# Attention by pairs of sequences, and token groups cut across all four sequences, in a fused attention and expert kernel

## The chip, the cores and the metric

The kernel runs on one core of one Trainium2 chip. The metric is device time in microseconds (us), from the first to the last instruction. All data are FP32. Lines such as L843 are line numbers of the kernel before.

## The reference

A decayed linear attention over blocks of a sequence feeds four experts that every token goes through, weighted by normalised probabilities. Cut to what matters:

```python
# q, k, v: (4, 8, 768, 64); lam: one decay per head
for b in range(nb):                                   # blocks of 64
    intra = einsum('bhic,bhjc->bhij', qb, kb) * Dmask     # lam ** (i - j), 0 above the diagonal
    out[:, :, sl] = einsum('bhij,bhjd->bhid', intra, vb) + einsum('bhid,bhde->bhie', qb * lam_pow, kv_state)
    kv_state = lam_block * kv_state + einsum('bhsd,bhse->bhde', kb * rev_pow, vb)
x = out.transpose(0, 2, 1, 3).reshape(3072, 512)      # token = sequence * 768 + position
p = domain_probs / (domain_probs.sum(-1, keepdims=True) + 1e-9)
for e in range(4):                                    # w1: (4, 512, 1024), w2: (4, 1024, 512)
    y += p[:, e:e + 1] * (maximum(x @ w1[e], 0) @ w2[e])
```

Sequences don't touch each other in attention, and tokens don't touch each other in the experts. So the tokens may be grouped in any way, as long as a sequence's chunks come in order.

## The kernel before

**Chunks and groups.** Attention uses chunks of 128 positions (C), six to a sequence (NCH), 24 in all. The kernel numbers them n = sequence * 6 + chunk. Eight consecutive chunks make a token group of 1024 tokens (CPG = 8, G = 1024), three groups in all (NG). A group's attention output lies turned in the tile xT, and the experts work on it while attention of the next group runs in between. The first group is sequence 0 and two chunks of sequence 1, and so on.

**Attention of a chunk** has three steps on TensorE. `turn(n)` transposes q and k of 8 heads (8 transposes, L529) into PSUM, ScalarE copies them out; from the second chunk of a sequence on, VectorE also scales q by the decay (qs). GpSimd decays k (`decayed`). `scores(n)` makes k q^T for 8 heads (L551), with two products side by side on 64 rows each, into two PSUM banks; VectorE masks them with the decay (two instructions, st<-sp). `values(n)` adds the state's part (L574, not for a first chunk), the values (L579) and makes the chunk's addition to the state (L587, not for a last chunk). These use halves of the array too. ScalarE copies the result into xT, VectorE updates the state kv, one for the sequence in hand. A product over FP32 is two records in the profile, so 8 products are 16 records; a transpose is one.

For eight of the chunks (`turn_across`), q and k are first re-laid in DRAM by small DMAs (`bring_across`, pieces let go one at a time by `trickle`, tensor across), so that VectorE's 32x32 transposes suffice and TensorE has nothing to turn.

**The experts** are products by a seven-multiplication scheme (M1 to M7) in two levels. A unit is one group with one expert, 12 in all; for each unit of the loop (`at`), `second_product` (L897, banks q..) of the present unit and `first_product` (L843, banks g1 and g3) of the next run interleaved in seven steps i, each in eight slots x. In the order SEQ the first products are M1, M5, M6, M2, M7, M3, M4. Each of the seven inner products of a first product fills g1 or g3 with four records, and VectorE (in M1 and M5 for four of them ScalarE) adds it to the tiles m; the next inner product into that bank waits for this. The last group (LAST) uses another nesting (L1123).

**What sets the order.** The schedule is manual: instructions run on each engine in the order written. Work of VectorE that is not urgent, sums of blocks above all, goes on the list `background`; `rest()` takes one item in each slot. Before, attention's VectorE work (masks, scaling, state) is put at the front of the same list by `soon`; in the first group it is done at once. Attention's steps lie in a list from which one is taken at x == 5 of each step and in some at x == 2 (L1483). `pump` lets out GpSimd's weight preparation (`chores`) and DMA stores at a pace; `feed` and `feed2` load operands on SyncE's queue a step or more ahead.

**Start and end.** The first group's attention has no experts to hide behind: a hand-written loop over i interleaves turn, scores and values of three consecutive chunks with first direct products (`direct_product`, L1253, tiles pM and pc). At the end, `give`, `give_across` and `turn_end` turn the last group's results back and store them.

**Memory.** Tiles of 128x512 for attention and experts share one pool of NPOOL = 47.

Of the kernel before, what the change touches and what calls it, by code (L numbers as in the profile page):

```python
# [17 lines left out]
NPOOL = 47  # L18
AHEAD = 2
# [3 lines left out]
def kernel(  # L23
# [30 lines left out]
    nc = tc.nc  # L54
# [53 lines left out]

    nat = {}

    def load(n, names="qkv"):

        b, c = divmod(n, NCH)
# [242 lines left out]
    ACROSS = {2: 2, 3: 2}  # L356
    across = dram.tile([B, 2, P, NHP, NCH * 4, 32], FP32, name="across")
    pieces = []

    def bring_across(b):  # L360
        c = ACROSS[b]
        for x, of in enumerate((q, k)):
            for y in range(4):
                for ac in range(NHP):
                    src = of[b, 4 * (y // 2) + ac, c * C:, (y % 2) * 32:(y % 2 + 1) * 32]
                    to = across[b, x, y * 32:(y + 1) * 32, ac, c * 4:]
                    pieces.append(lambda to=to, src=src: nc.sync.dma_start(
                        out=to, in_=src.rearrange("(t p) d -> p t d", p=32),
                    ))

    def trickle(m=1):
        for _ in range(m):
            if pieces:
                pieces.pop(0)()

    def comes_across(n):
        b, c = divmod(n, NCH)
        return b in ACROSS and c >= ACROSS[b]

    def load_across(n):  # L380
        b, c = divmod(n, NCH)
        for x, name in enumerate("qk"):
            t = small(f"{name}x")
            nc.sync.dma_start(
                out=t[:].rearrange("p (h c) -> p h c", c=C),
                in_=across[b, x, :, :, c * 4:c * 4 + 4].rearrange("p h t d -> p h (t d)"),
            )
            nat[n, name + "x"] = t

    def load_more(n):  # L390
        if not comes_across(n):
            load(n)
        else:
            trickle(len(pieces))
# [5 lines left out]
    for n, names in ((0, "qk"), (1, "qk"), (0, "v"), (2, "qk"), (1, "v"), (3, "qk")):  # L400
        load(n, names)
    raw_w1(0, "A11")
    load(2, "v")
    load(3, "v")
# [39 lines left out]
    kv = consts.tile([P, NHP, D], FP32, name="kv")  # L444
# [17 lines left out]
    def turn_gates():  # L462
        p, o = bank("s0", "gp"), small("gr")
        n = CPG * E
        nc.tensor.transpose(out=p[0:n, 0:P], in_=gate[:, LAST * CPG:].rearrange("p n e -> p (n e)"), identity=ident[:])
# [9 lines left out]
    background = []  # L475
    aside = []
# [17 lines left out]
    def soon(n, *work):  # L494

        background[0:0] = work
        if n < CPG:
            rest(len(work))
# [7 lines left out]
    def turn_across(n):  # L506

        qT, kT, kn = nat.pop((n, "qx")), nat.pop((n, "kx")), nat[n, "k"]
        qs = small("qs") if n % NCH else None

        def scaled():
            if n % NCH:
# [4 lines left out]
        if n % NCH < NCH - 1:  # L517
            decayed(kn)

    def turn(n, tags):  # L520
# [15 lines left out]
        if n % NCH:  # L536
# [3 lines left out]
        if n % NCH < NCH - 1:  # L540
            decayed(kn)

    def scores(n, tags):
        while n not in turned:
            rest(force=True)
        qT, kT, _ = turned[n]

        sp = [bank(tags[r], "sp") for r in range(2)]
        for ac in range(NHP):
            for r in range(2):  # L550
                nc.tensor.matmul(  # L551
                    out=sp[r][:, ac * C:(ac + 1) * C], lhsT=hc(kT)[half[r], ac], rhs=hc(qT)[half[r], ac],
                    start=True, stop=True,
                )
        st = [small("st") for _ in range(2)]

        def mask(hd):
            tt(nc.vector, st[hd][:], sp[hd][:], s_decay[:, hd].rearrange("p h c -> p (h c)"), ALU.mult)

        soon(n, *(lambda hd=hd: mask(hd) for hd in range(2)))  # L560
        masked[n] = st

    def values(n, tags):
        kn, vn = nat.pop((n, "k")), nat.pop((n, "v"))
        qs = turned.pop(n)[2]
        st = masked.pop(n)
        c = n % CPG
        first, last = n % NCH == 0, n % NCH == NCH - 1

        op = [bank(tags[r], "op") for r in range(2)]  # L570
        heads = [(a, r, c) for a in range(2) for r in range(2) for c in range(2)]
        if not first:
            for a, r, x in heads:
                nc.tensor.matmul(  # L574
                    out=op[r][half[x], a * C:(a + 1) * C], lhsT=kv[half[r], 2 * a + x], rhs=hc(qs)[half[r], 2 * a + x],
                    start=(a == 0), stop=False, skip_group_check=True,
                )
        for a, r, x in heads:
            nc.tensor.matmul(  # L579
                out=op[r][half[x], a * C:(a + 1) * C], lhsT=vn[:, 4 * r + 2 * a + x], rhs=hc(st[r])[:, 2 * a + x],  # L580
                start=(first and a == 0), stop=True, skip_group_check=True,
            )
        kvp = op[1][:, 2 * C:].rearrange("p (h d) -> p h d", d=D)
        if not last:
            for ac in range(NHP):
                for r in range(2):
                    nc.tensor.matmul(  # L587
                        out=kvp[half[r], ac], lhsT=kn[:, 2 * ac + r], rhs=vn[:, 4 * r + ac], start=(ac == 0), stop=True,
                        skip_group_check=True,
                    )  # L590
        for r in range(2):
            nc.scalar.copy(
                out=xT[:, 2 * r:2 * r + 2, c * C:(c + 1) * C],
                in_=op[r][:, 0:2 * C].rearrange("p (a t) -> p a t", t=C),
            )
        if not last:
            def state():
                if first:
                    nc.vector.tensor_copy(out=kv[:], in_=kvp)
                else:  # L600
                    tt(nc.vector, kv[:], kv[:], q_decay[:, :, C - 1:C].to_broadcast([P, NHP, D]), ALU.mult)
                    tt(nc.vector, kv[:], kv[:], kvp, ALU.add)

            soon(n, state)

    def attention(g):

        steps = []
        early, late = prepare_x(g)
        for n in range(g * CPG, (g + 1) * CPG):  # L610
            steps.append(lambda n=n: turn(n, ("s0", "s1")))
            steps.append(lambda n=n: scores(n, ("s0", "s1")))

            def end(n=n):
# [3 lines left out]
                values(n, ("s0", "s1"))  # L618
                if n + AHEAD < B * NCH:
                    load_more(n + AHEAD)  # L620
                if n == g * CPG + CPG // 2 - 1:
                    chores[0:0] = early
                if n == g * CPG + CPG - 1:
                    chores.extend(late)
            steps.append(end)
        return steps


    hid = {}
# [44 lines left out]
    LAST = NG - 1  # L674
# [207 lines left out]
    def second_product(g, e, m, banks):  # L882

        def part(sj, s):
# [23 lines left out]
            o, x, w = a[:, j * DH:(j + 1) * DH], p[:, s * DH:(s + 1) * DH], gate[:, n, e:e + 1]  # L908
# [5 lines left out]
            if e == E - 1 and m in ("M2", "M4", "M5", "M3"):  # L914
                results.append(lambda: nc.sync.dma_start(out=out[n * P:(n + 1) * P, j * DH:(j + 1) * DH], in_=o))
# [91 lines left out]

    RESULT = {"M2": (0, 0), "M3": (0, 1), "M4": (1, 0), "M5": (1, 1)}

    def give(m, t, tags, dds=(0, 1)):  # L1010
# [5 lines left out]
        for x, dd in enumerate(dds):  # L1016
# [6 lines left out]
        r, d = LAST * G + j * W + t * 256, i * DH + dds[0] * P  # L1023
        nc.sync.dma_start(
            out=out[r:r + 256, d:d + w].rearrange("(s p) d -> p s d", p=P),
# [5 lines left out]
    def give_across(m, dd, t):  # L1031
# [7 lines left out]
        nc.vector.transpose(out=o[:, t * 256:(t + 1) * 256], in_=sums[m][:, 2 * dd + t])  # L1039
        r, d = LAST * G + j * W, i * DH + dd * P  # L1040
        for a in range(4 * t):
            by = nc.scalar if a == 1 else nc.sync
            by.dma_start(
                out=out[r:r + W, d + a * 32:d + (a + 1) * 32].rearrange("(b p) d -> p b d", p=32),
                in_=o[a * 32:(a + 1) * 32].rearrange("p (b d) -> p b d", d=32),
            )
# [40 lines left out]
    def turned_product(t, h, w):  # L1087
# [9 lines left out]
        r = LAST * G + j * W + t * 256  # L1097
# [420 lines left out]
```

## Time and profile before

| | |
|---|---|
| time, median of 3 runs (lowest, highest) | 1186.49 us (1186.17, 1189.06) |
| span of the profiled execution | 1183.3 us |
| granted TensorE clock | 1.000 |
| scores of all chunks, L551, records, busy | 256 + 128, 18.6 + 9.3 us |
| values, L579 | 384 records, 26.7 us |
| state's part, L574 | 320 records, 13.3 us |
| addition to the state, L587 | 320 records, 12.7 us |
| transposes of q and k, L529 | 128 records, 19.3 us |
| first products, L843, largest form | 1960 records, 469.8 us |
| masks st<-sp on VectorE | 48, mean 680 ns |
| scaling qs<-qT and qs<-qx | 12 of 938 ns, 8 of 791 ns |
| 128x512 sum on VectorE with one PSUM input, m<-pg,m | mean 687 ns |
| DMA engines' mean busy share between 90 and 560 us | 0.91 to 0.93 |

Busy is the time in which at least one record of the group was running; records overlap, so a matmul's length (mean 279 ns for L579) is more than the distance to the next. To see what a group costs TensorE, compare the start of its first record with the start of the first record after it. In the timeline, xN is the number of records merged into one line; brackets at the end of a line give idle time before it and what ended it, and a line without brackets had none.

### The profile page before, as it was taken

How to read it: one execution, taken by the hardware profiler on the slowest of the kernel's cores; microseconds unless marked ns; L12 is line 12 of the kernel's file. 1: busy time of each engine (PE TensorE's matmuls, PEld its weight loads, DVE VectorE, ACT ScalarE, POOL GpSimd, SP SyncE). 2: the span in 40 equal slices, each digit the busy share in tenths (PEclk: the TensorE clock that was granted, in tenths of full speed). 3: DMA queues.
4: the chain of work that ended last, by engine and by line, in shares of the span. 5: the costliest groups of instructions: out<-in, count | busy, mean ns of one | idle time of the engine just before them, and what ended most of it. 6: DMA issues, size and time to landing. Idle time of an engine off the chain costs nothing.

```text
span 1183.3 us, 17880 instructions
## 1 busy us (share of the span) xinstructions
PE 1175.7 (99%) x6559; PEld 1022.7 (86%) x6559; DVE 790.7 (67%) x1333; ACT 274.0 (23%) x500; POOL 628.7 (53%) x600
## 2 busy tenths in 40 slices
PE   9999999999999999999999999999999999999998
PEld 8888888888888888888888888888888888888887
DVE  6785785567468857647856774773665676777785
ACT  3332122112211201211220120121243342341331
POOL 2756258349457900055244655416584693783884
PEclk9999999999999999999999999999999999999999
DMA  9797799999999997899998989998986657566543
GB/s 232 194 292 238 250 300 310 362 326 333 353 359 334 328 291 227 262 287 303 303 317 247 295 287 318 275 312 294 316 289 238 261 196 272 212 237 248 213 155 95
DMA packets 265608, 324.23 MB, mean 274 GB/s; under 512 B 121489, under 2 KB 206897, under 8 KB 265521
## 3 DMA queue, kind: packets, MB, share of 16 engines
q1 hardware_dynamic: 254912, 320.27, 81.6%
q10 hardware_dynamic: 10608, 2.82, 1.1%
q8 instruction: 52, 0.85, 0.3%
q14 instruction: 36, 0.29, 0.1%
HBM read 237.69 MB, written 89.54 MB: 277 GB/s over the span
## 4 chain that ended last, share of the span: by engine, by line
PE 94%; DVE 3%; DMA 2%; issue 0%; POOL 0%; SPq 0%; ACT 0%; DVEq 0%
PE pg L843 38%; PE q L897 32%; PE pq L1123 13%; PE pM L1253 2%; PE op L579 2%; PE sp L551 2%; PE pc L1253 2%; DMA w_ops<-ops 2%; PE op L574 1%; PE op L587 1%; DVE sums L95 0%; PE qp L529 0%; PE kp L529 0%; PE pg L1123 0%; DVE acc L95 0%; DVE m L95 0%
## 5 line engine op out<-in xcount | busy, mean ns | idle before, releaser
L843 PE MATMUL pg<-xs_in,ws_in 128*128 128x256 f32 x1960 | 469.8, 380 | 0.9 <-DVE m L95 0.9
L843 PEld LDWEIGHTS pg<-xs_in,ws_in 128*128 128x128 f32 x1960 | 371.2, 190 | 52.9 <-DVE m L95 2.3
L95 DVE TENSOR_TENSOR m<-pg,m 128x512 f32<-128x512 f32 x451 | 308.1, 687 | 106.5 <-PE pg L843 99.6
L897 PE MATMUL q<-w2t,hS 128*128 128x256 f32 x1024 | 243.4, 380 | 0.0
L897 PEld LDWEIGHTS q<-w2t,hS 128*128 128x128 f32 x1024 | 193.2, 190 | 27.0 <-issue 0.2
L913 DVE SCALAR_TENSOR_TENSOR acc<-q,gate,acc 128x256 f32<-128x256 f32 x192 | 92.5, 482 | 170.2 <-PE q L897 170.0
L897 PE MATMUL q<-w2t,m 128*128 128x256 f32 x768 | 182.7, 381 | 0.0
L897 PEld LDWEIGHTS q<-w2t,m 128*128 128x128 f32 x768 | 144.8, 190 | 20.5 <-issue 0.3
L855 ACT ACTIVATE m<-m 128x512 f32<-128x512 f32 x132 | 83.0, 630 | 283.6 <-DVE m L95 276.6
L95 POOL TENSOR_TENSOR m<-m,xT 128x512 f32<-128x512 f32 x64 | 80.7, 1276 | 71.6 <-ACT m L855 53.9
L95 POOL TENSOR_TENSOR kn<-kn,s_decay 128x512 f32<-128x512 f32 x20 | 22.5, 1126 | 140.7 <-PE kp L529 134.8
L95 DVE TENSOR_TENSOR sums<-pq,sums 128x256 f32<-128x256 f32 x153 | 64.2, 422 | 46.0 <-PE pq L1123 38.8
L851 ACT COPY m<-pg 128x512 f32<-128x512 f32 x88 | 51.6, 586 | 174.3 <-PE pg L843 173.4
L1123 PE MATMUL pq<-acc,w2t 128*128 128x256 f32 x352 | 86.6, 379 | 0.0
L95 POOL TENSOR_TENSOR ops<-w2b 128x256 f32<-128x256 f32 x24 | 17.9, 766 | 119.4 <-DMA w2b<-in_moe_w_dram 111.3
L1123 PEld LDWEIGHTS pq<-acc,w2t 128*128 128x128 f32 x352 | 66.8, 190 | 9.3 <-issue 0.3
L95 POOL TENSOR_TENSOR acc<-hT,hT 128x512 f32<-128x512 f32 x32 | 40.3, 1274 | 30.3 <-PE pq L1123 28.4
L95 POOL TENSOR_TENSOR w2o<-w2b 128x512 f32<-128x512 f32 x32 | 40.6, 1291 | 23.3 <-DMA w2b<-in_moe_w_dram 23.3
L786 ACT ACTIVATE m<-m 128x512 f32<-128x512 f32 x44 | 27.7, 630 | 101.8 <-DVE m L95 101.8
L95 DVE TENSOR_TENSOR hS<-m,m 128x512 f32<-128x512 f32 x56 | 45.3, 812 | 4.9 <-ACT m L855 4.9
L95 DVE TENSOR_TENSOR m<-m,m 128x512 f32<-128x512 f32 x56 | 47.2, 844 | 0.0
L95 POOL TENSOR_TENSOR acc<-hT,acc 128x512 f32<-128x512 f32 x32 | 40.7, 1273 | 7.4 <-PE pq L1123 5.4
(158 smaller groups left out, 1360.4 us busy)
## 6 DMA issues: line engine op xcount, KB each, us to landing
xs_in<-x_ops SPq DMA_DIRECT2D x70, 896.0 KB, 6.4
ws_in<-w_ops SPq DMA_DIRECT2D x70, 896.0 KB, 8.7
w2t<-w_ops SPq DMA_DIRECT2D x66, 256.0 KB, 6.8
w2t<-w_sums SPq DMA_DIRECT2D x64, 256.0 KB, 3.9
w_ops<-ops SPq DMA_DIRECT2D x28, 512.0 KB, 5.5
w2t<-in_moe_w_dram SPq DMA_DIRECT2D x48, 256.0 KB, 3.4
w2b<-in_moe_w_dram SPq DMA_DIRECT2D x32, 256.0 KB, 5.9
w_sums<-w2o SPq DMA_DIRECT2D x16, 512.0 KB, 5.1
```

The lines of the kernel that those rows point to most:

```text
L95: eng.tensor_tensor(out=o, in0=a, in1=b, op=op)
L551: nc.tensor.matmul(out=sp[r][:, ac * C:(ac + 1) * C], lhsT=hc(kT)[half[r], ac], rhs=hc(qT)[half[r], ac], start=True, stop=True,)
L574: nc.tensor.matmul(out=op[r][half[x], a * C:(a + 1) * C], lhsT=kv[half[r], 2 * a + x], rhs=hc(qs)[half[r], 2 * a + x], start=(a == 0), sto ...
L579: nc.tensor.matmul(out=op[r][half[x], a * C:(a + 1) * C], lhsT=vn[:, 4 * r + 2 * a + x], rhs=hc(st[r])[:, 2 * a + x], start=(first and a = ...
L786: nc.scalar.activation(out=o[:], in_=o[:], func=AF.Relu)
L843: nc.tensor.matmul(out=p[:, j * 256:(j + 1) * 256], lhsT=ws[i][:, j * P:(j + 1) * P], rhs=xs[i], start=(fresh and j == 0), stop=True, skip ...
L851: nc.scalar.copy(out=new[at][:], in_=p[:])
L855: nc.scalar.activation(out=new[at][:], in_=new[at][:], func=AF.Relu)
L897: nc.tensor.matmul(out=p[:, s * DH:(s + 1) * DH], lhsT=h[A_OF[m]][:, c * 256 + s * P:c * 256 + (s + 1) * P], rhs=fed2[g, e, m][uu][:, c], ...
L913: nc.vector.scalar_tensor_tensor(out=o, in0=x, scalar=w, in1=o, op0=ALU.mult, op1=ALU.add)
L1123: nc.tensor.matmul(out=p[:, 0:256], lhsT=fed3[e, m, x // 2][:, x % 2, c * P:(c + 1) * P], rhs=b[B_OF[i]][:, c * 256:(c + 1) * 256], start= ...
L1253: nc.tensor.matmul(out=p[:, s * 256:(s + 1) * 256], lhsT=a[c][:, f:f + P], rhs=b[:, c, j * 256:(j + 1) * 256], start=(s == 0 and c == 0 an ...
```

## The change

Two chunks at the same position of two sequences now go through attention as one step. For this the token groups are cut the other way: a group holds two chunk positions of all four sequences. `where(n)` gives chunk position and sequence of step number n, `token(n)` its first token. The state kv is kept for all four sequences. The group's order is chunk 0 of sequences 0 to 3, chunk 1 of sequences 0 to 3; in the last group it is chunks 4 and 5 of sequences 0 and 1, then of 2 and 3.

`scores` makes the scores of both chunks in one run of 16 products; in groups 1 and 2 the second chunk's go to g3 and g1, the first products' banks. `values` makes the state's parts of both, the values of both, and both additions to the state (into a bank of their own, g3 in groups 1 and 2), with one copy to xT of twice the width for each half and one update of the state for both. Masks and state updates have a list of their own, `lately`, from which one item is taken in each slot, besides the one of `background`; two of the four masks are issued at once. The places of the steps are written down (AT), in (step, slot) counted over all units. The start's loop is written anew for pairs. The chunks that go through DRAM are now positions 4 and 5 of all sequences, in pieces of half the size. Gates and result stores follow the new token order, and the pool has one tile less.

```diff
-NPOOL = 47
+NPOOL = 46
+    def where(n):
+        g, x = divmod(n, CPG)
+        half, x = divmod(x, 4)
+        return (2 * g + x // 2, 2 * half + x % 2) if g == LAST else (2 * g + half, x)
+    def token(n):
+        c, b = where(n)
+        return b * S + c * C
...
-    across = dram.tile([B, 2, P, NHP, NCH * 4, 32], FP32, name="across")
+    SECOND = NCH - 2
+    across = dram.tile([2, P, NHP, B, 8, 32], FP32, name="across")
...
-    for n, names in ((0, "qk"), (1, "qk"), (0, "v"), (2, "qk"), (1, "v"), (3, "qk")):
+    for n, names in ((0, "qk"), (1, "qk"), (0, "v"), (1, "v")):
         load(n, names)
     raw_w1(0, "A11")
-    load(2, "v")
-    load(3, "v")
+    for n, names in ((2, "qk"), (3, "qk"), (2, "v"), (3, "v")):
+        load(n, names)
...
-    kv = consts.tile([P, NHP, D], FP32, name="kv")
+    kv = consts.tile([P, B, NHP, D], FP32, name="kv")
...
     def soon(n, *work):
-        background[0:0] = work
         if n < CPG:
-            rest(len(work))
+            for f in work:
+                f()
+        else:
+            lately.extend(work)
...
+    def scores(n, *tags):
+        for m in (n, n + 1):
+            while m not in turned:
+                take(lately, True)
+        masks = []
+        for m, pair in zip((n, n + 1), tags):
+            qT, kT, scaled[m] = turned.pop(m)
+            sp = [bank(pair[r], "sp") for r in range(2)]
             for ac in range(NHP):
                 for r in range(2):
...
+        if n < CPG:
+            for f in masks[0] + masks[1]:
+                f()
+        else:
+            for f in masks[1]:
+                f()
+            soon(n, *masks[0])
...
+        if not first:
+            for i, m in both:
+                for a, r, x in heads:
+                    nc.tensor.matmul(
+                        out=place(i, a, r, x), lhsT=kv[half[r], b + i, 2 * a + x], rhs=hc(qs[m])[half[r], 2 * a + x],
+                        start=(i == 0 and a == 0), stop=False, skip_group_check=True,
+                    )
+        for i, m in both:
+            for a, r, x in heads:
+                nc.tensor.matmul(
+                    out=place(i, a, r, x), lhsT=vn[m][:, 4 * r + 2 * a + x], rhs=hc(st[m][r])[:, 2 * a + x],
+                    start=(first and i == 0 and a == 0), stop=True, skip_group_check=True,
+                )
...
+    AT = 4, 8, 13, 17, 24, 29, 34, 39
...
+        for n in range(g * CPG, (g + 1) * CPG, 2):
+            at = AT[(n - CPG) // 2]
+            steps.append((at - 2, 1, lambda n=n: load_more(n)))
+            steps.append((at - 1, 1, lambda n=n: load_more(n + 1)))
+            steps.append((at, 2, lambda n=n: turn(n, ("s0", "s1"))))
+            steps.append((at, 5, lambda n=n: turn(n + 1, ("s0", "s1"))))
+            steps.append((at, 7, lambda n=n: scores(n, ("s0", "s1"), ("g3", "g1"))))
...
+                values(n, ("s0", "s1", "g3"))
...
+            steps.append((at + 1, 7, end))
...
-        nc.vector.transpose(out=o[:, t * 256:(t + 1) * 256], in_=sums[m][:, 2 * dd + t])
+        for x in range(2):
+            at = (2 * x + t) * P
+            nc.vector.transpose(out=o[:, at:at + P], in_=sums[m][:, 2 * dd + t, x * P:(x + 1) * P])
...
+    between = {
+        1: ((m1[0], m1[2]), ()), 2: ((m2[0],), (m1[1], m1[3])), 3: ((m2[2],), (m2[1],)),
+        4: ((m2[3],), (quarter_5(0), quarter_5(2))),
+    }
+    last_pair = CPG // 2 - 1
+    for i in range(last_pair + 2):
...
+        if i > 0:
+            step(lambda: scores(2 * i - 2, pairs[2], pairs[0]))
+        if i == 1:
+            step(lambda: values(2 * i - 2, (*pairs[0], pairs[1][0])), *between[i][0])
+        if i <= last_pair:
+            for x in range(2):
+                step(lambda: turn(2 * i + x, pairs[1 + x]))
...
+        if i > 1:
+            step(*between[i][0], lambda: values(2 * i - 2, (*pairs[0], pairs[1][0])), lambda: None)
...
-                if steps and (at > 0 or i > 1) and (x == 5 or (x == 2 and i in (1, 3, 5) and at not in (0, 3))):
-                    steps.pop(0)()
+                while steps and (at * 7 + i, x) == steps[0][:2]:
+                    steps.pop(0)[2]()
+                take(lately)
```

## The prediction

> **What bounds the kernel now.** I read the engine sums first, then the chain that ended last, then TensorE's own waits, then single stretches of the timeline. The page:
>
> ```profile
> PE 1175.7 (99%) x6559; PEld 1022.7 (86%) x6559; DVE 790.7 (67%) x1333; ACT 274.0 (23%) x500; POOL 628.7 (53%) x600
> PEclk9999999999999999999999999999999999999999
> PE 94%; DVE 3%; DMA 2%; issue 0%; POOL 0%; SPq 0%; ACT 0%; DVEq 0%
> ```
>
> TensorE is busy in 1175.7 of 1183.3 us at the full clock, and 94% of the last chain is its own. So the end moves only with what TensorE issues, or with a wait it does not have now. Its waits:
>
> ```profile
> PE pg L843 <- DVE m L95: 1.1, 3, 0.5
> PE zp L413 <- DVE xT L408: 1.1, 1, 1.1
> PE qp L529 <- DMA qn<-in_q_dram: 0.6, 1, 0.6
> PE pc L1253 <- DVE xt L95: 0.4, 1, 0.4
> PE op L579 <- DVE st L95: 0.2, 1, 0.2
> ```
>
> There is almost nothing to take from waits. What attention costs TensorE is seen in the timeline of TensorE around one chunk's scores and one chunk's values (start, length, line, records):
>
> ```profile
> 139.11 1.03 PE L843 MATMUL pg<-xT,w1b 128*128 128x256 f32 x4
> 140.07 1.16 PE L551 MATMUL sp<-qT,kT 64*128 64x128 f32 x16
> 141.16 1.99 PE L897 MATMUL q<-w2t,hS 128*128 128x256 f32 x8
> 142.99 1.03 PE L843 MATMUL pg<-xT,ops 128*128 128x256 f32 x4
> ...
> 153.35 1.03 PE L843 MATMUL pg<-xt,w1o 128*128 128x256 f32 x4
> 154.31 0.67 PE L574 MATMUL op<-qs,kv 64*64 64x128 f32 x16
> 154.91 1.09 PE L579 MATMUL op<-st,vn 128*64 128x128 f32 x16
> 155.83 0.63 PE L587 MATMUL op<-vn,kn 128*64 128x64 f32 x16
> 156.40 1.99 PE L897 MATMUL q<-w2t,m 128*128 128x256 f32 x8
> 158.23 1.03 PE L843 MATMUL pg<-xt,ops 128*128 128x256 f32 x4
> ```
>
> Compare starts, not lengths. Four pg records take 0.86 us elsewhere in this view, here 0.96 (139.11 to 140.07). Eight q records take 1.73, here 1.83 (141.16 to 142.99). Each change of the shape of the array costs about 0.10 us, once before and once after. In the single records of the 1.09 us of scores, the pairs start 0.112 apart except the first and the last, 0.21 each.
>
> [...] 0.09 to 0.10 us at each of these borders, none between the full-size products. [...] the trace before never lends the products' banks in steady state. [...] a 128x512 sum of two SBUF tiles means 844 ns, one with a PSUM input 680 to 690.
>
> **The change, part by part.** The multiplication count is the same: 24 chunks, 16 turned on TensorE, 8 through DRAM, 4 first and 4 last chunks.
>
> *Fewer mode changes.* Scores save, for each second chunk of a pair, 0.09 entry + 0.10 first pair + 0.10 last pair + 0.10 on the first q record = 0.39. Values save 0.09 + 0.09 (L574 to L579) + 0.10 + 0.10 and two steps of 0.05 = 0.48. That is 0.87 a pair, 8 pairs in groups 1 and 2: 7.0 us. Lower bound, only the borders with the products vanish: 0.4 a pair, 3.2.
>
> *Moved work.* The first group now holds 4 first chunks, not 2, so 2 chunks' L574 (0.46 net) go to later groups, and 1 chunk's L587 (0.48) comes back: +0.4 later, already counted in the start below.
>
> *The start (to the first pc, 61.67 us before).* It is now nearly serial. With VectorE's decay table done at 10.7 (its row starts at 7.31 and lasts 3.40), as before, four masks of 0.64 end at 13.3; values of pair 0, which follow the scores directly, end at 15.0 and not earlier: about 1.3 us of idle TensorE. The two direct quarters then run to 18.6, turns 2 and 3 to 20.4, and scores 2, in the banks of turn 3, wait for ScalarE's four copies of 0.59, to 21.9: 1.4 idle. From there, by durations of the rows before: scores and turns to 25.6, a quarter, values, two quarters to 34.0, scores 4, turns, a quarter to 39.8, values 4 to 43.8, a quarter and scores 6 to 47.8, a quarter and values 6 to 53.8, four quarters to 60.8, 0.3 of waiting for T2: 61.1, so -0.5. The four saved mode changes pay for the idle. The masks of pair 4 stand behind four own sums on VectorE (5.3 us before) and have 0.5 us to spare; GpSimd's eighth decay has 2.5. If either is late: +1 to +3.
>
> *VectorE bursts (a new wait).* Before, mask, scale and state went to the front of one list of which one item is taken in a slot, so they put off the sums. Now they have a list of their own (lately) besides, and two of the four masks are issued at once, because the second chunk's scores lie in g3 and g1, the banks of the next product. Queued behind them on VectorE are the evacuations of that product; TensorE waits for those. After scores, masks end about 1.5 us later, and g1 is wanted after 1.9: no wait there. The damage is in the third and fifth matmuls of the product. VectorE's load by product differs; its timeline shows the heaviest kind, the one after M7, in unit 5:
>
> ```profile
> 672.66 1.11 DVE L95 TENSOR_TENSOR m<-m,m 128x512 f32<-128x512 f32 x1
> 673.70 1.28 DVE L95 TENSOR_TENSOR m<-pg,m 128x512 f32<-128x512 f32 x2
> 674.90 1.25 DVE L95 TENSOR_TENSOR m<-m,m 128x512 f32<-128x512 f32 x1
> 676.08 0.47 DVE L913 SCALAR_TENSOR_TENSOR acc<-q,gate,acc 128x256 f32<-128x256 f32 x1
> ```
>
> No idle is printed there: 7 evacuations of 0.60 (two take 1.28), 4 accumulations of 0.40 and 8 sums of 0.65 or more are 11 us of a product of 13 (4 x 1.73 + 7 x 0.86 on TensorE). Two of the eight score steps (4 and 39) fall in front of such a product. I follow the queue: with 3 masks of 0.6 ahead, M6 waits 0.5, M4 0.2, M5 1.1, M2 0.2 us at step 4, where four xt sums are queued as well: 2.1. At step 39, 0.7. Before M7 (steps 17 and 24) 0.35 each. Before M6 and M1 (8, 13, 29, 34), where ScalarE evacuates or no sums are queued, about 0. Together 3.5; low 1, and with the GpSimd lengths above (1.1 to 1.3 a sum) 7. One wait of before, 0.57 at 383 us behind a state update, goes: -0.6.
>
> *The rest.* across moves the same 4 MB in 128 pieces instead of 64, spread over 30 products; behind them on SyncE's queue stand the feeds, which land 6 to 9 us after issue with 13 us given: hidden. One pool tile less makes loads wait for VectorE more often: hidden unless a feed is late, 0 to 2. Twelve instead of six result stores of half the size on SyncE and eight small transposes instead of four near the end: four before take 1.5 us, I add 0.2 (0 to 0.8). Gate copies: eight on VectorE, each like the 64x4 copy of q_decay (154 ns), 1.2 us in unit 4, hidden under the product.
>
> Sum: -7.0 + 0.4 - 0.5 + 3.5 - 0.6 + 0.2 = -4.0, so 1186.5 - 4.0 = 1182.5 us.
>
> **Rivals.**
> A. The mode changes are saved and VectorE keeps up: bursts cost 1, not 3.5. For it: VectorE is 67% busy, and products ran without TensorE waiting although evacuations began up to 1.5 us late (starts of m<-pg against the ends of the matmuls they read). Against: at steps 4 and 39 the sum exceeds the product. -6.5 to -8: 1179.5.
> B. VectorE and not TensorE bounds the products after scores, bursts cost 6 to 7: -1: 1185.5. For it: sums of 1.1 to 1.3 us next to GpSimd. Against: scores and values themselves give VectorE 2.1 and 4 us in which no product runs.
> C. Slower: the start is late by 3 (masks behind own sums, decays behind weight sums), a full pool holds a load and the feed behind it for 2, bursts cost 7: +4 to +6: 1191. For it: the start is serial and was dense. Against: each chain above ends before it is wanted.
>
> **How the numbers follow.** Forecast (-2 to -6) 0.45, A 0.22, B 0.19, C 0.14. Faster than 1182.9 are A and 0.7 of the forecast's cases, 0.54; within 0.3% the rest of the forecast and nearly all of B, 0.31; slower 0.15. The range goes from below A's value, 1177.5, to 1188.5, between B and C, which leaves out most of C and the edge of A.
>
> **What would show it.** Score groups of 32 records in about 1.98 us and not 2.18; the number of borders halved; TensorE's waits for VectorE at pg grown from 1.1 to about 4 to 5 us, mostly in the products after steps 4 and 39; the first pc between 60.5 and 62.5. Wrong if the group of 32 takes twice the time of 16, if TensorE waits for DMA, or if the first pc comes after 64.

## The result and the profile after

| | before | after |
|---|---|---|
| time, median (lowest, highest), 5 runs each | 1186.53 us (1186.17, 1189.06) | 1198.11 us (1192.17, 1201.79) |
| span of the profiled execution | 1183.3 us | 1198.9 us |
| ratio after to before, 95% interval | | 1.0089 (1.0061 to 1.0117) |

The changed kernel is slower by 0.9%, and its runs spread over 9.6 us against 2.9. Line numbers from here on are those of the changed kernel unless said otherwise. Its page, engine sums, clock and chain of work that ended last:

```profile
PE 1175.7 (98%) x6559; PEld 1027.4 (86%) x6559; DVE 785.8 (66%) x1327; ACT 270.3 (23%) x476; POOL 632.1 (53%) x600
PEclk9999999999999999999999999999999999999999
PE 55%; DMA 1%; DVE 1%; ACT 0%; issue 0%; DVEq 0%; SPq 0%
```

TensorE's busy time is the same to the tenth, in a span 15.6 us longer. So TensorE is idle for as much longer, and the chain has lost its one owner (94% before). (That the busy time stays is a balance: the saved mode changes take about 6 us out of it, and slow records after the idle times put about 5 back; both are worked out below.) TensorE's waits after (what waited, what it waited for, us in total, times, longest):

```profile
PE pg L884 <- DMA ws_in<-w_ops: 10.1, 4, 4.6
PE pg L884 <- DMA w2b<-in_moe_w_dram: 2.6, 1, 2.6
PE gp L476 <- DVE gn L475: 2.0, 1, 2.0
PE op L612 <- DVE st L94: 1.3, 2, 1.1
```

Before, no row of this view named a feed. Now first products wait 12.7 us for xs_in and ws_in, the operands that `feed` loads for each product (the second row names w2b, but ws_in landed at 841.95 us and the wait ended at 842.09), and the transpose of the gates waits 2.0 us for the new copies gn. A wait for VectorE's m, which the prediction had priced at 3.5 us, has no row; starts of records show short ones all the same, as the timeline below does once. The mode changes, those of the array's shape, were saved as forecast. TensorE's timeline of the changed kernel around a pair's scores and values:

```profile
155.71 1.02 PE L884 MATMUL pg<-xt,ops 128*128 128x256 f32 x4
156.67 2.06 PE L570 MATMUL sp<-qT,kT 64*128 64x128 f32 x32
158.66 1.99 PE L938 MATMUL q<-w2t,hS 128*128 128x256 f32 x8
...
162.46 1.89 PE L938 MATMUL q<-w2t,hS 128*128 128x256 f32 x8
164.38 1.10 PE L884 MATMUL pg<-ops 128*128 128x256 f32 x4
...
172.61 1.10 PE L606 MATMUL op<-qs,kv 64*64 64x128 f32 x32
173.65 1.97 PE L612 MATMUL op<-st,vn 128*64 128x128 f32 x32
175.44 1.10 PE L620 MATMUL kvp<-vn,kn 128*64 128x64 f32 x32
176.47 1.99 PE L938 MATMUL q<-w2t,hS 128*128 128x256 f32 x8
```

From the first score to the first q record it is 1.99 us for 32 records, against 1.09 for 16 before. The eight q records from 162.46 to 164.38 take 1.92 us, where 1.73 is usual: the first product's next record waited for VectorE, whose sum of m ended at 164.23. The large waits stand elsewhere, in the same timeline at 327 and 343 us:

```profile
327.22 1.96 PE L884 MATMUL pg<-xs_in,ws_in 128*128 128x256 f32 x8 [2.44 <-DMA ws_in<-w_ops]
329.02 1.89 PE L938 MATMUL q<-w2t,hS 128*128 128x256 f32 x8
...
342.94 3.42 PE L884 MATMUL pg<-xs_in,ws_in 128*128 128x256 f32 x8 [2.53 <-DMA ws_in<-w_ops]
346.15 2.17 PE L938 MATMUL q<-w2t,hS 128*128 128x256 f32 x8
```

Eight records after the first idle take 1.80 us, start to start; after the second 3.21. The second idle cost its own length and then about 1.5 us more at half pace, the first its length alone; the last section comes back to it. By starts of records, TensorE stood 0.71, 2.60, 2.69 and 4.77 us before a feed between 270 and 450 us, 2.77 at 839, and 2.17 before the gates: 15.7 us.

Why was a feed late? SyncE's timeline of the changed kernel ahead of the second of these waits (start, length of the issue, what is loaded):

```profile
317.53 0.35 SPq L797 DMA_DIRECT2D xs_in<-x_ops  x1
317.92 0.43 SPq L799 DMA_DIRECT2D ws_in<-w_ops  x1
318.76 1.33 SPq L133 DMA_DIRECT2D qn<-in_q_dram  x2
320.19 2.76 SPq L133 DMA_DIRECT2D kn<-in_k_dram  x2
323.00 3.98 SPq L128 DMA_DIRECT2D vn<-in_v_dram  x1
327.03 1.46 SPq L376 DMA_DIRECT2D across<-in_q_dram  x2
...
332.45 1.57 SPq L919 DMA_DIRECT2D w2t<-w_sums  x2
334.11 0.46 SPq L797 DMA_DIRECT2D xs_in<-x_ops  x1
334.62 0.49 SPq L799 DMA_DIRECT2D ws_in<-w_ops  x1
```

There is no gap: SyncE issues without a pause, single issues of 0.4 to 4 us. The feed issued at 334.6 lands 7.7 us after the end of its issue, no later than others: from 200 to 450 us the mean for ws_in from the end of issue to landing is 8.9 us before and 8.2 after. What is late is the issue. Whether SyncE is ahead or behind shows in its own waits in that stretch. Where it is ahead, it waits for TensorE to free a w2t tile (L878 before, L919 after). Before:

```profile
SPq L878 <- PE q L897: 24.3, 16, 7.4
```

After:

```profile
SPq L376 <- DMA ws_in<-w_ops: 7.7, 3, 3.2
SPq L186 <- POOL ops L94: 4.1, 8, 1.1
SPq L187 <- DMA ws_in<-w_ops: 4.1, 2, 2.3
SPq L919 <- PE q L938: 4.0, 9, 0.7
```

SyncE had 24.3 us in hand and now has 4.0. In the same 250 us it issued 228 DMAs in 166.0 us before and 271 in 184.8 after (lengths of issues added up from its timeline; waits that fall inside an issue, some 17 and 22 us, are in them); 66 of the 271 are pieces of the across copy, 32 KB each and 46.7 us in all, where before had 16 of 64 KB, all after 400 us. The DMA engines' share was near 1 there before too (0.99 from 200 to 300 us, 1.02 from 300 to 350).

### The profile page after: what moved, and what is told of

It reads as the page before. It is cut to its first block, busy times and chain, and to the rows that moved or that the text cites. A ratio compares the mean times of both kernels' runs of the same rounds, so it can differ in the third digit from the quotient of the medians.

```text
span 1198.9 us, 17951 instructions
## 1 busy us (share of the span) xinstructions
PE 1175.7 (98%) x6559; PEld 1027.4 (86%) x6559; DVE 785.8 (66%) x1327; ACT 270.3 (23%) x476; POOL 632.1 (53%) x600
## 4 chain that ended last, share of the span: by engine, by line
PE 55%; DMA 1%; DVE 1%; ACT 0%; issue 0%; DVEq 0%; SPq 0%
PE pg L884 24%; PE q L938 15%; PE pq L1169 13%; DMA xs_in<-x_ops 1%; PE op L612 0%; DVE sums L94 0%; PE pg L1169 0%; PE sp L570 0%; PE pM L1105 0%; DMA w2b<-in_moe_w_dram 0%; PE op L606 0%; PE yp L1063 0%; PE yp L1138 0%; DVE y L1086 0%; DVE hS L94 0%; DVE st L94 0%
## 5 line engine op out<-in xcount | busy, mean ns | idle before, releaser
L884 PE MATMUL pg<-xs_in,ws_in 128*128 128x256 f32 x1960 | 474.0, 382 | 12.9 <-DMA ws_in<-w_ops 10.1
L94 POOL TENSOR_TENSOR ops<-w1o 128x256 f32<-128x256 f32 x32 | 27.8, 887 | 32.7 <-PE pg L884 17.3
```

What stands on the lines that cost most here:

```text
L94: eng.tensor_tensor(out=o, in0=a, in1=b, op=op)
L884: nc.tensor.matmul(out=p[:, j * 256:(j + 1) * 256], lhsT=ws[i][:, j * P:(j + 1) * P], rhs=xs[i], start=(fresh and j == 0), stop=True, skip ...
```

## Experiments

The theory after this reading: the across copy, whose pieces now go out one at a time from 75 to 540 us, falls into a stretch in which SyncE's queue and the DMA engines have nothing left, and holds the feeds up. The rival: it is the loads of q, k and v, which now come in pairs in adjacent products. Ratios are to the kernel before, in the same session.

**Across copy at the times of before.** The pieces of sequences 0 and 1 two a slot from the start, the others from the fourth unit.

```diff
-    for b in range(B):
+    for b in range(2):
         bring_across(b)
...
-                trickle()
+                trickle(2)
...
+        if at == 3:
+            bring_across(2)
+            bring_across(3)
```

> The changed kernel, with the pieces of the across copy at the times of the kernel before: those of the first two sequences at twice the rate from the start, those of the other two from the fourth unit on, so that almost none is issued from 200 to 400 us. Theory (the pieces spread over a stretch in which the DMA engines are full hold up the feeds): the waits for xs_in and ws_in between 270 and 450 us (0.7, 2.6, 2.7, 4.8 us in the profiled run) go, and with them some 3 us of half-pace matmuls after them: 1184 to 1188 us. Rival (the loads of a pair of chunks in two adjacent products hold them up): the waits stay, 1196 to 1200 us.

1204.15 us (1202.71 to 1205.19), ratio 1.0147 (1.0134 to 1.0160), slower than either expectation. The waits between 270 and 430 us are all gone, but a single one of 10.1 us stands at 435 and another of 5.3 at 538. SyncE's queue there:

```profile
413.35 0.43 SPq L797 DMA_DIRECT2D xs_in<-x_ops  x1
413.83 0.42 SPq L799 DMA_DIRECT2D ws_in<-w_ops  x1
...
417.39 2.98 SPq L133 DMA_DIRECT2D kn<-in_k_dram  x2
420.46 2.47 SPq L128 DMA_DIRECT2D vn<-in_v_dram  x1
422.98 2.47 SPq L376 DMA_DIRECT2D across<-in_q_dram  x2
...
436.25 0.43 SPq L797 DMA_DIRECT2D xs_in<-x_ops  x1
```

22.9 us lie between two feeds, and SyncE issues for 9.8 of the 11 us from 425 to the second, while the DMA share is 0.64. So where the pieces go, the waits go; and SyncE's queue can hold a feed with the DMA engines not full.

**Loads of a pair set apart.**

```diff
-            steps.append((at - 2, 1, lambda n=n: load_more(n)))
+            steps.append((at - 3, 1, lambda n=n: load_more(n)))
```

> The changed kernel, with the load of the first chunk of a pair three products ahead of its turn in place of two, so that a product without loads lies between the two loads. Theory (across pieces): the waits stay, within 2 us of 1198. Rival (bunched loads): the waits at 324, 340 and 443 us go, 1185 to 1189 us. The longer life of three tiles may hold a load up; it would show as SyncE waiting for a tile.

1196.49 us, ratio 1.0080 (1.0067 to 1.0093), not told apart from the change itself. Waits of 2.3, 1.6, 3.4 and 0.7 us for feeds stay (266, 328, 431 and 447 us). The rival alone doesn't carry it.

**The kernel before with the across copy spread** (three runs). First, pieces at half rate and the fourth sequence's from the third unit on:

```diff
-        if at == 3:
+        if at == 2:
             bring_across(3)
...
-                if x % 2:
+                if x % 4 == 3:
                     trickle()
```

> The kernel before, with its across pieces (64 of 64 KB) at half their rate from the first unit on and those of the fourth sequence from the third unit on, so that 200 to 400 us carries about the bytes that the changed kernel has there. Theory (across pieces in a full stretch): feeds come late between 250 and 420 us, 5 to 12 us slower, 1191 to 1198. Rival (bunched loads, which this kernel does not have): within 1.5 us of 1186.5.

1207.96 us, ratio 1.0179 (1.0166 to 1.0192), but not for the reason asked about. `load_more` lets out all pieces left before the first load that needs one, and so 29 of 64 KB were issued in a row:

```profile
314.52 0.32 SPq L758 DMA_DIRECT2D ws_in<-w_ops  x1
...
317.78 12.66 SPq L367 DMA_DIRECT2D across<-in_q_dram  x13
330.48 10.71 SPq L367 DMA_DIRECT2D across<-in_k_dram  x16
```

TensorE waited 17.5 us for the feed behind them. It shows in the other kernel that a row of pieces holds a feed, and nothing about the size. The next run halves only the third sequence's rate, so that its pieces last until about 250 us:

```diff
-                if x % 2:
+                if x % (4 if at < 3 else 2) == 1:
                     trickle()
```

> The kernel before, with two pieces of the third sequence's across copy a product in place of four, so that they last to the thirteenth product (about 250 us) rather than the sixth; the fourth sequence's as before. Theory (issues and short packets in a stretch that is already full delay the feeds): waits of 1 to 4 us between 200 and 270 us, 1188 to 1192. Rival (only the pairing of the loads delays feeds): 1186 to 1187.5.

1187.15 us, ratio 1.0007 (0.9999 to 1.0015): the rival's number.

In the third, only the fourth sequence's pieces move, and a load lets out only those of its own and earlier sequences:

```diff
-            trickle(len(pieces))
+            trickle(sum(b <= n // NCH for b, _ in pieces))
...
-        if at == 3:
+        if at == 2:
             bring_across(3)
...
-                if x % 2:
+                if x % (4 if at >= 2 else 2) == 1:
                     trickle()
```

> The kernel before, with the fourth sequence's across copy issued from the third unit on, two pieces of 64 KB a product (about 300 to 480 us) in place of four a product from the fourth unit on (400 to 510 us). The loads stay one chunk at a time. Theory (issues of the across copy in SyncE's queue in the full stretch are enough to delay feeds): waits for feeds between 300 and 420 us of 3 to 10 us in sum, 1190 to 1197. Rival (it takes the pair of loads as well): under 1.5 us of waits, 1186 to 1188.

1189.68 us (1185.46 to 1193.18), ratio 1.0021 (1.0012 to 1.0030): a small loss and a wider spread, between the two expectations. Before carries these pieces at a cost of about 2.5 us. They are a milder load than the change's: 22 issues of 64 KB from 200 to 450 us, against 66 of 32 KB.

**No across copy, in either kernel.**

```diff
-                in_=across[x, :, :, b, (c - SECOND) * 4:(c - SECOND) * 4 + 4].rearrange("p h t d -> p h (t d)"),
+                in_=(q, k)[x][b, 0:4, 4 * C:6 * C].rearrange("h (p t) d -> p h (t d)", p=P),
...
-            trickle(sum(b <= where(n)[1] for b, _ in pieces))
...
-    for b in range(B):
-        bring_across(b)
```

> The changed kernel without the across copy: none of its 128 pieces is issued, and the loads from it take rows of q and k as they lie, so the last two chunk positions see wrong queries and keys; the loads keep their bytes and packet length. Theory (the pieces' traffic in the stretch from 200 to 450 us makes the feeds late): feed waits before 450 us under 2 us in sum, 1184 to 1187; the gate wait (2.2) and what the lane costs at 833 us may stay in that. Rival (the pairs' loads are enough): feed waits of 5 us or more stay, 1190 to 1197.

> The kernel before without the across copy, in the same way (wrong queries and keys where they came across). It has no feed waits to lose, so every theory has it within 2 us of 1186.5. It is the yardstick for the run above: what is left of the change when neither kernel copies across. By the prediction's sum without its VectorE term that is 5 to 7 us less for the changed kernel, plus its gate wait of 2.

Changed kernel 1185.29 us (1183.39 to 1188.33), ratio 0.9994 (0.9986 to 1.0002); kernel before 1186.63, ratio 1.0006 (0.9998 to 1.0015). This settles whether it is the copy: it costs the changed kernel 0.95% (1.0089 less 0.9994), some 11 us, and the kernel before nothing that can be told from noise. What is left of the change without it is about 1 us of gain (0.9994 against 1.0006, at the edge of noise). No feed is waited for before 800 us. SyncE's waits from 200 to 450 us in the changed kernel without the copy:

```profile
SPq L918 <- PE q L937: 49.3, 26, 8.3
SPq L186 <- POOL ops L94: 15.0, 13, 4.6
```

It is 49.3 us ahead, with the pairs' loads in adjacent products as in the change. So the pairs need no help once the pieces are gone. The smaller pool is no rival either: loads waited 9.2 us for a tile here, 4.4 in the changed kernel with the copy and 1.5 in the kernel before.

**By which resource?** The issues moved to ScalarE's queue, all else kept; and the same bytes in packets of 1 KB instead of 128 bytes.

```diff
-                    pieces.append((b, lambda to=to, src=src: nc.sync.dma_start(
+                    pieces.append((b, lambda to=to, src=src: nc.scalar.dma_start(
```

> The changed kernel, with the 128 issues of the across copy in ScalarE's DMA queue in place of SyncE's; bytes, packets and times of issue stay. Theory (the feeds stand in SyncE's queue behind the issues ahead of them; that queue is the limit): SyncE's issuing falls from 21 to 23 of 25 us to under 18 in the stretches at 250 to 350 and 425 us, the waits for xs_in and ws_in between 270 and 450 us (10.8 us) and the slow matmuls after them (about 3) go: 1184 to 1187 us. Rival (the DMA engines themselves are full, whoever issues): the waits stay, 1196 to 1200 us. A second rival, that ScalarE's evacuations come late behind its issues: waits for ACT m of 0.5 to 1 us each, 1187 to 1195.

1192.76 us, ratio 1.0060 (1.0047 to 1.0073). Waits for feeds fall from 12.7 to 4.0 us in this view of the two profiles. SyncE issues for 125.3 us in the stretch, not 184.8, yet it isn't ahead:

```profile
SPq L187 <- DMA ws_in<-w_ops: 8.7, 2, 4.7
SPq L919 <- DMA xs_in<-x_ops: 5.8, 2, 3.4
SPq L250 <- DMA ws_in<-w_ops: 5.1, 2, 3.4
SPq L919 <- PE q L938: 4.9, 6, 2.5
```

Its time now goes into waits for earlier DMAs that these lines share no tile with. The semaphores in the changed kernel's trace show how that can come about: its 1065 issues, 15 of them ScalarE's, take eight of them in turn (1045 of 1064 times the next in one fixed order), 1047 wait for the semaphore that they will raise themselves, and none ended before the DMA ahead on it had landed. In the run with the moved issues SyncE waited 3.9 us at L186 (w_ops<-ops) for a piece that ScalarE had issued, and from 200 to 450 us 98.3 us for earlier DMAs to land, against 45.9 in the changed kernel. So a piece can hold up SyncE's issues whichever queue issues it; no run took that away alone.

One issue is short beside its DMA: 0.7 us for a piece in the changed kernel from 200 to 450 us (mean of 66), and the piece lands 4.5 us after its end (median). By the medians moving all of them was worth 0.29%, 3.4 of the 11 us, but the two intervals overlap. What the rest is due to, the transfers, the turns of the semaphores or ScalarE's own work coming late (TensorE waits 1.2 us for it at 218 us), is not shown.

```diff
-                    src = of[b, 4 * (y // 2) + ac, SECOND * C:, (y % 2) * 32:(y % 2 + 1) * 32]
+                    t = (SECOND + y % 2) * C
+                    src = of[b, 4 * (y // 2) + ac, t:t + C]
...
-                        out=to, in_=src.rearrange("(t p) d -> p t d", p=32),
+                        out=to.rearrange("p t d -> p (t d)"), in_=src.rearrange("(p t) d -> p (t d)", p=32),
```

> The changed kernel, with each piece of the across copy of the same bytes, but in 32 runs of 1 KB in place of 256 of 128 bytes: it leaves out the change of order, so the last two chunk positions see wrong queries and keys. As many issues in SyncE's queue. Theory (SyncE's queue, by the number of issues): most of the waits stay, 1193 to 1199 us. Rival (time of the DMA engines on short packets): the waits between 270 and 450 us go, 1184 to 1188 us; issues then get shorter too, and the DMA share of the windows at 200 to 400 us falls below 0.95.

1197.80 us, ratio 1.0099 (1.0083 to 1.0116): no gain, with as many issues and bytes. Short packets aren't the cost.

**The gate wait, and sums of edits.** In the first run the gate load is moved too; it then comes after sums that read it, so they use another expert's gates.

```diff
-            if nests and i == 2:
+            if nests and i == 4:
                 nc.scalar.dma_start(
                     out=gate_bc,
```

> The changed kernel, with the eight copies of gate columns made at the end of the first group's sums in place of beside the transpose, and the broadcast load of the gates at the fifth product of its unit in place of the third. Both theories: the wait of the gate transpose at 508 us (2.2) goes, and the feed at 833 us no longer stands behind the broadcast load (2.8, and about 1.3 of half-pace matmuls after it): 1191 to 1193 us. The rival (that the waits are taken up elsewhere, since the next feed is late anyway): 1196 to 1199.

1196.44 to 1206.72 us in five runs and 1216.10 in a sixth, ratio 1.0114 (1.0089 to 1.0139): inconclusive, as both edits moved other waits. The copies alone, in both runs as below, here with the across issues on ScalarE:

```diff
     def gates():
...
+        for i in range(CPG):
+            t = token(LAST * CPG + i) // P
+            nc.vector.tensor_copy(out=gn[:, i * E:(i + 1) * E], in_=gate[:, t])
```

> The kernel with the across copy in ScalarE's queue, and the eight copies of gate columns at the end of the first group in place of beside the transpose. Theory: 2.2 us less than the run with the across copy alone moved, 1182 to 1185, below the kernel before. Rivals: as there, less 2.2; or 0 less, if the next feed is late anyway.

1193.01 us, ratio 1.0069 (1.0050 to 1.0089), nothing gained. The eight copies take 5.0 us from 76 us on, where they took 0.65 beside the transpose, and TensorE waits 3.5 us for VectorE behind them. Next, loads apart and gate copies by ScalarE in two instructions, with the across issues on ScalarE (first run below), and also one piece a slot from the group's direct products on, by ScalarE or by SyncE:

```diff
-        for i in range(CPG):
-            t = token(LAST * CPG + i) // P
-            nc.vector.tensor_copy(out=x[:, i * E:(i + 1) * E], in_=gate[:, t])
+        by_chunk = gate.rearrange("p (b c) e -> p c b e", b=B)
+        for y in range(2):
+            nc.scalar.copy(
+                out=x[:, y * 4 * E:(y + 1) * 4 * E].rearrange("p (c b e) -> p c b e", c=2, b=2),
+                in_=by_chunk[:, 2 * LAST:2 * LAST + 2, 2 * y:2 * y + 2],
+            )
...
-            if m in SEQ0[-2:]:
-                trickle()
+            trickle()
```

> The changed kernel with across issues in ScalarE's queue (from the same slots as in the changed kernel), loads of a pair two products apart, gate columns copied by ScalarE in two instructions. Theory (the gains add): 1192.8 less 2.5 for the gates less 1 for the loads, 1188 to 1190, still not below the kernel before. Rival (waits move to the next feed): 1192 to 1195.

> The changed kernel with four edits: across issues in ScalarE's queue, one piece a slot from the first unit's direct products on (where the DMA share is 0.6 to 0.8), the two loads of a pair two products apart, and the gate columns copied by ScalarE in two instructions in place of VectorE in eight. Theory: the feed waits and the gate wait go but for about 2 us, and the 6 us that the fewer mode changes save show: 1181 to 1184, faster than the kernel before. Rival (the DMA engines are full from 200 to 450 us, so the feeds of a pair's loads stay late): 1186 to 1190.

> As the run with the four edits, but with the across issues left in SyncE's queue. Theory (SyncE's queue): feed waits of 3 to 8 us between 200 and 350 us come back, 1186 to 1191. Rival (it is enough to have the pieces earlier and the loads apart): within 1 us of the run with four edits.

1193.57 (ratio 1.0060), 1201.01 (1.0118) and 1194.32 us (1.0067). Gains that were measured one by one don't add: the gate wait is gone in all three, and feeds are late by 8 to 10 us in sum. The second is the worst: ScalarE's copies stand behind the pieces, and TensorE waits 5.9 us at 82 us.

Last, the pieces in two halves, each where its own limit has room: sequences 0 and 1 early by SyncE, 2 and 3 from the 24th product (about 430 us) on by ScalarE.

```diff
-                    pieces.append((b, lambda to=to, src=src: nc.sync.dma_start(
+                    pieces.append((b, lambda to=to, src=src, by=nc.sync if b < 2 else nc.scalar: by.dma_start(
...
+            if at * 7 + i == 23:
+                bring_across(2)
+                bring_across(3)
```

> The changed kernel with the first two sequences' across pieces at twice the rate from the start in SyncE's queue, the other two's from about 430 us on (two a slot) in ScalarE's queue, and the gate columns copied by ScalarE. Theory (two limits: full DMA engines from 200 to 430 us, SyncE's queue from 400 to 520 us): feed waits before 560 us under 3 us in sum, 1183 to 1187. Rival (a burst of pieces costs the same wherever it stands): waits of 5 us or more near 430 to 540 us, 1190 to 1200.

1189.96 us (1188.46 to 1192.87), ratio 1.0035 (1.0025 to 1.0046). Feed waits before 560 us are 0.6 us in sum, as expected, and SyncE waits 52.7 us for TensorE from 200 to 450 us; the time is 3 us over the expected range's end, with these waits left:

```profile
PE pg L887 <- DMA ws_in<-w_ops: 3.5, 3, 2.1
PE gp L479 <- ACT gn L475: 2.7, 1, 2.7
```

Two more runs take the gate wait away, the second with loads apart too:

```diff
+        if at == 2:
+            chores.append(pick_gates)
```

> As the run with the pieces in two halves, but the gate columns are copied in the third unit, some 100 us before they are turned. Theory (the wait of 2.7 us at 494 us is lost time): 1187 to 1188. Rival (it is slack that the feeds after it use): 1189.5 to 1191.

> The same with the loads of a pair two products apart. Theory (with the DMA engines still full between 200 and 430 us, loads that do not follow each other leave the feeds more room): 0 to 1.5 us less, 1186 to 1188. Rival (no effect or, by tiles held longer, later loads): 1187 to 1190.

1195.33 us (1191.87 to 1199.63) and 1189.00 us (1185.81 to 1194.66, ratio 1.0018, 1.0004 to 1.0033). The first is slower than without the edit, with 4.5 us for a feed at 439 us: which feed is late changes with anything in the order. No version with the copy in place beat the kernel before; whether one exists stays open.

## Why the prediction was wrong

- **The step that failed** is in "The rest": "behind them on SyncE's queue stand the feeds, which land 6 to 9 us after issue with 13 us given: hidden." The landing was right (8.2 us). The 13 us were counted from an issue at its usual time; but the issue stood in a queue that had waited 24 us for TensorE over 250, and there it was given 50 more pieces of 0.7 us. This was priced at 0. It cost 10.1 us of waits up to 450 us and about 3.4 at half pace after two of them.
- **One more feed was late**, at 839 us, and this is not the copy, whose last piece went out at 530 us. The issue of ws_in stood until 833.28 us on a semaphore that the broadcast load of the gates held; that load was issued at 824.90 and landed at 833.27. The wait was 2.6 us, with about 1.5 at half pace. The prediction has no term for it.
- **Gate copies**, "hidden under the product": 160 ns each, as forecast, but a TensorE instruction waits for them and they stand behind VectorE's other work: 2.0 us.
- **VectorE bursts**, 3.5: 1.9. By the starts of records a first product's record came 0.2 to 0.4 us late six times, and under 0.1 twice; three of the six lie in the product after step 4 (0.8 us, where 2.1 was forecast). Three such waits of before, 2.0 us in sum, are gone, where the forecast had counted on 0.6. So the net is 0, not 2.9.
- **Fewer mode changes**, 7.0, less 0.4 of moved work: right. From the start of the last product record ahead of each group of scores or values to the start of the second one behind it, less 0.216 us for each of these two, it is 54.5 us in the kernel before (32 groups, from 75 us on) and 48.4 in the changed one (16): 6.2 less.
- **The start**, -0.5: first pc at 62.45 us, +0.8 against 61.67. The idle of 1.3 us before the first values was there (1.12 and 0.16); a late q of chunk 5 added 0.6.
- **The wait at 383 us**, -0.6, is gone, as forecast.

With the measured terms, by starts of records: -6.2 for mode changes, +1.9 and -2.0 for VectorE, +0.8 for the start, +2.2 for the gates, +0.2 at the end, +13.5 ahead of feeds and about +5.2 of slow records after these waits make 15.6 us, the difference of the spans. Without the feeds and what follows them it is about -3. That this is near -4.0 is luck: VectorE came out 3 us better than forecast, the gates and the start 3.5 us worse. The rivals had slower at 1191 from the start, a full pool and VectorE; the loss came from none of the three. The text named TensorE waiting for DMA as what would make it wrong.

## What to carry to other kernels

A transfer that is hidden has two margins: from issue to landing, and how far its issuing queue is ahead. Read the second from that queue's waits for the consumer in the stretch in question: 24 us in hand there were the budget, and with 50 more small DMAs 4 were left, though the DMA engines' mean share from 200 to 450 us was 0.98 in both kernels. When a change moves where small DMAs fall, count them by stretch, and not only their count or bytes over the whole. Each took 0.7 us to issue here, one of eight semaphores until it had landed 4.5 us later (median), and a part of the time of DMA engines that were at 0.98; which of these weighs most stays open.

## What the runs showed of the hardware

TensorE came back at half pace after some of its idle times, but not after every one of a length. The granted clock in the traces says when; the page's row PEclk is too coarse for it. In the changed kernel it is 1.00 or 0.50 from 80 us on, and 0.50 lasts 3.41 us each of three times before the products end: from 343.29, 449.10 and 841.63 us, 31 and 115 steps of 3.41 us apart. Each of these stretches began right after a step of that grid in which TensorE had been idle for 2.53, 2.83 and 2.15 us; after the other steps, with up to 1.77 us of idle, none began. In the kernel before no idle time was over 0.49 us between 80 and 1175 us, and the clock stayed at 1.00. The idle of 2.60 us that ended at 327.22 is cut in two by the grid, at 326.22 (1.44 and 1.00 us by the view below), and the clock stayed; the one of 2.69 that ended at 342.94 lies in one stretch (PE busy, PEld, DVE, ACT, POOL, then PEclk, DMA share and GB/s):

```profile
322.81:326.22 3.41, 1.97 (x10) 1.39 (x8) 0.48 (x1) 0.59 (x1) 1.65 (x2) 1.00 1.02 385
326.22:329.63 3.41, 2.41 (x11) 2.18 (x12) 1.10 (x2) 0.00 (x0) 0.00 (x0) 1.00 0.93 203
339.88:343.28 3.40, 0.87 (x5) 0.47 (x4) 1.21 (x3) 0.00 (x0) 0.00 (x0) 1.00 1.09 326
343.29:346.70 3.41, 3.41 (x10) 2.70 (x9) 1.00 (x2) 0.00 (x0) 0.00 (x0) 0.50 0.87 246
```

In the slow stretches records start 0.427 us apart and not 0.216, 1.5 to 1.8 us in all for each of the three. The changed kernel's spread goes with it: its five runs, from the fastest to the slowest, had mean clocks of 0.999, 0.999, 0.997, 0.996 and 0.995.

A VectorE copy of 128x4 took 0.16 us each of eight times at 510 us, with GpSimd idle; in the run with the copies moved the eight took 4.97 us from 76.08 us on. In the changed kernel a 128x24 scaling at 72.55 us took 1.21 us and ended 0.03 us after the end of a 128x512 GpSimd sum; in the run with four edits it took 0.18. VectorE's 128x512 sums of two SBUF tiles (m and hS from m and hS, 168 in the changed kernel) took at most 0.69 us where no GpSimd instruction ran meanwhile (77 of them), and 0.91 on average, up to 1.70, where one did. The 451 sums m<-pg,m, with one input in PSUM, took 0.69 in both cases.

An issue of a 256 KB load of v took 0.37 us at 436 us in the run with two halves and 3.98 us at 323 us in the changed kernel.
